# One kernel for a decaying recurrence and a gated feed-forward: its table of emission times replaced by a list scheduler, and five d_ff tiles beside the recurrence instead of four

## The chip, the cores and the metric

The kernel runs on 1 core of one Trainium2 chip. The metric is the device time of one execution in microseconds (us). Engine names in the profile: PE is TensorE's matmuls, PEld its weight loads, DVE VectorE, ACT ScalarE, POOL GpSimd, SP SyncE, which here issues the DMAs.

## The reference, cut to what matters

```python
# batch 4, 8 heads, 768 tokens, head dimension 40
for t in range(S):
    y[:, :, t] = np.einsum('bhd,bhde->bhe', rt, state)
    Sa = np.einsum('bhde,bhe->bhd', state, at)
    state = state * wt[:, :, None, :] - np.einsum('bhd,bhe->bhde', Sa, bt)
    state = state + np.einsum('bhd,bhe->bhde', vt, kt)
x = y.transpose(0, 2, 1, 3).reshape(3072, 320)
out = ((x @ w_a) * (x @ w_b)) @ w_out      # d_ff = 1536
```

The three weight matrices arrive as float64.

## The kernel before, in words

**The recurrence** ("attention") goes in 12 chunks of 64 tokens, each for 4 batches. The state passes from chunk to chunk, so the chunks' last parts come one after the other. Per chunk the stages are:

- `prep(n, b)` for each batch (L416): load the packed input `I`, two scans and `BK` on DVE, products on POOL, the transposed form `psn` and the scores `pssc` on PE, the masked scores into `TT` on DVE; behind the last batch the diagonal blocks of `TT` go out to DRAM (`nb_d`).
- `lanes(n)` (L491): the diagonal blocks of all 32 heads come back as `N`, laid over the partitions, and 31 pairs of DVE instructions (`Yt` on L504, `Y` on L507), each dependent on the one before, solve them; the result goes out through `ts_d`.
- `merge(n)` (L522): the result comes back into `TT`, and two rounds of small matmuls (`psw`, `pst`) with ACT copies give the block beside the diagonal.
- `loads(n, b)` (L556) and `main(n, b)` (L566): per batch a chain of PE products with an ACT or DVE copy behind each (`psr`, `RH`, `psu`, `UV`, `psut`, `pss`, `psg`, `G`, `psy`, `yn`, `psyt`, `xT`), with the state's update in it (`tmp` on DVE, `ST` on POOL, `psst` on PE).
- `xform(n)` (L666): the chunk's x for 256 tokens, as high and low parts (`xk`), for the feed-forward; also stored to DRAM (`xk_d`).

**The feed-forward** goes in 12 tiles of 128 of the 1536 columns (d_ff tiles). One tile for one chunk's 256 tokens is a unit, so there are 144: 16 `ab` matmuls, an ACT copy `asb`, the product `g` on DVE, its high part `gh` on ACT and low part `gl` on POOL, and later 6 `po` matmuls (`Moe.first` L312, `Moe.second` L333). The weights' float64 words are decoded to high and low parts piece by piece, six pieces to a tile (`wraw`, with DVE, ACT and POOL work; `decode` L219, `weights` L277); a last pair of DMAs (`fill_rows` L271) completes a tile's `wt`.

Four d_ff tiles (`F1 = 4`) run beside the attention, for chunks 0 to 10: 44 units. Their sums go out to DRAM (`po_d`). The other 8 tiles follow in groups of two over all chunks, for which each chunk's `xk` is loaded again (`xk2_n`, 720 KB) and its sums too (`acc`, 320 KB). The first two `xk2` and one group's weights get room on the pool of the preparation once that is done (`early` L783), the others on the pools of the attention (`late` L799), with loads spread in time (`l0`, `l1`).

**The order.** Each engine keeps the instructions in the order in which the program emits them (`InOrder`, L51), and what waits holds up what stands behind it on that engine. The order of emission comes from the table `DEF` of emission times, 16 units to a chunk: each stage of each part is put in a list of events with its time (`at` L709, `staged` L712), which is then sorted. The lanes' DVE instructions are an exception: they wait in a queue, and one is put behind each other DVE instruction (`fill_one`, L723). PSUM has four banks for the attention (`ps_at`), two for `ab` and two for `po`. In the profile almost all instructions have the line of the helper that issues them, L62.

Of the kernel before, what the change touches and what calls it, by code (L numbers as in the profile page):

```python
# [38 lines left out]
DEF = {  # L39
# [8 lines left out]
}  # L48


class InOrder:  # L51
    """An engine whose instructions keep the order in which they are given; after() comes
    behind each."""

    def __init__(self, tc, eng):
        self.tc, self.eng, self.after = tc, eng, None

    def __getattr__(self, name):
        fn = getattr(self.eng, name)

        def call(*args, **kwargs):
            r = fn(*args, **kwargs)  # L62
            self.tc.keep_in_program_order(r)
            if self.after:
                self.after()
# [16 lines left out]
    # identity for the rows of each head  # L82
# [67 lines left out]
def wkv_moe(ctx, tc, pin, rv, vn, wa, wb, wo, out):  # L150
    nc0 = tc.nc
    nc = types.SimpleNamespace(**{e: InOrder(tc, getattr(nc0, e)) for e in (
        "tensor", "vector", "scalar", "gpsimd", "sync")})
# [21 lines left out]
    # start values of the scans: 1 at the first column of each group and behind the last  # L175
# [4 lines left out]
    # strict mask s < t, on both halves of the partitions  # L180
# [7 lines left out]
    # 1 where the row belongs to head j of its group  # L188
# [11 lines left out]
    # rows of the identity: lane half p holds the rows s = 2 i + p  # L200
# [11 lines left out]
    # DRAM scratch  # L212
# [6 lines left out]
    def decode(pool, raw, rows, ncol, dst_hi, dst_lo):  # L219
        """High and low parts of float64 words, or of float32 values."""  # L220
        def t(name, dt=I32):
            return pool.tile([P, 192], dt, tag=name, name=name, bufs=2)[:rows, 0:ncol]
# [4 lines left out]
        if not WIDE:  # L227
            yield
            nc.scalar.copy(out=dst_hi, in_=shaped(raw))
            nc.vector.tensor_sub(out=dst_lo, in0=shaped(raw), in1=dst_hi.bitcast(F32))  # L230
            yield
        low, high = raw[:, :, 0], raw[:, :, 1]
        ex, mt, rs = t("w_ex"), t("w_mt"), t("w_rs")
# [6 lines left out]
        # what lies below the first 21 bits, in units of 2^-51 of the power of two  # L240
        ts(out=rs, in0=low, scalar1=1, scalar2=None, op0=ALU.logical_shift_right)
        yield
# [3 lines left out]
        stt(out=rf, in0=rs, scalar=2.0 ** -51, in1=ex.bitcast(F32), op0=ALU.mult, op1=ALU.mult)  # L246
        nc.gpsimd.tensor_sub(out=shaped(f), in0=shaped(f), in1=dst_hi.bitcast(F32))
        nc.gpsimd.tensor_add(out=dst_lo, in0=shaped(f), in1=shaped(rf))
        yield
# [3 lines left out]
    def load_piece(f, j, h):  # L253
        """Half of the columns of a d_ff tile of w_a, w_b or w_out."""
# [4 lines left out]
        if WIDE:  # L259
            raw = stage.tile([P, 192, 2], I32, tag="wraw", name="wraw", bufs=3)[:rows, 0:ncol]  # L260
            nc.sync.dma_start(out=raw.rearrange("p c x -> p (c x)"), in_=src.bitcast(I32))
        else:
            raw = stage.tile([P, 192], F32, tag="wraw", name="wraw", bufs=3)[:rows, 0:ncol]
# [3 lines left out]
    def weight_tiles(pool, i, bufs=1):  # L267
        return (pool.tile([PK, 2, 6, P], F32R, tag=f"wt{i}", name=f"wt{i}", bufs=bufs),
                pool.tile([P, 2, DM], F32R, tag=f"wo{i}", name=f"wo{i}", bufs=bufs))

    def fill_rows(wt):  # L271
        # rows of heads 6 and 7 that meet the low parts of x
# [4 lines left out]
    def weights(dest):  # L277
        """All d_ff tiles in turn, a piece per step; a step ends one piece, begins the next
        and loads the one after."""
        pieces = [(f, j, h) for f in range(NF) for j, h in PIECES]  # L280
        raw, begun = load_piece(*pieces[0]), None
        for i, (f, j, h) in enumerate(pieces):
            yield
            if begun:
                next(begun)
            following = load_piece(*pieces[i + 1]) if i + 1 < len(pieces) else None
            wt, wot = dest(f)
            if j < 2:
                v = wt[:, j, :, h * C:(h + 1) * C]
                begun = decode(stage, *raw, v[:, 0:3], v[:, 3:6])  # L290
            else:
                v = wot[:, :, h * (DM // 2):(h + 1) * (DM // 2)]
                begun = decode(stage, *raw, v[:, 0], v[:, 1])
            next(begun)
            raw = following
            if (j, h) == PIECES[-1]:
                yield
                next(begun)
                begun = None
                fill_rows(wt)  # L300
        yield
# [3 lines left out]
    class Moe:  # L305
        """Runs d_ff tiles for 256 tokens at a time; the second product of a tile comes after
# [686 lines left out]
```

## Time and profile before

| | |
|---|---|
| time, median of 3 runs | 1033.35 us (1030.91 to 1040.08) |
| span of the profiled execution, the only time its page gives | 1042.0 us |
| busy: PE, DVE, POOL, ACT | 88%, 66%, 41%, 39% |
| until chunk 3's main starts | 0 to 257.5 us |
| mains of chunks 3 to 10 | 257.5 to 668.4 us |
| main of chunk 11 | 668.4 to 725.9 us |
| seam: two more groups of instructions on PE, then PE idle from 755.0 | 725.9 to 771.2 us |
| units with nothing beside them | 771.2 to 1033.0 us |

The page cuts the span in slices; the trace can be asked for each engine's busy time in any stretch, with the clock that TensorE was granted (1.00 is full speed) and what the DMA engines moved. The stretches above were cut where the first `psr` of a chunk starts, where the last `xT` ends, and where PE stops and starts at the seam.

### The profile page before, as it was taken

How to read it: one execution, taken by the hardware profiler on the slowest of the kernel's cores; microseconds unless marked ns; L12 is line 12 of the kernel's file. 1: busy time of each engine (PE TensorE's matmuls, PEld its weight loads, DVE VectorE, ACT ScalarE, POOL GpSimd, SP SyncE). 2: the span in 40 equal slices, each digit the busy share in tenths (PEclk: the TensorE clock that was granted, in tenths of full speed). 3: DMA queues.
4: the chain of work that ended last, by engine and by line, in shares of the span. 5: the costliest groups of instructions: out<-in, count | busy, mean ns of one | idle time of the engine just before them, and what ended most of it. 6: DMA issues, size and time to landing. Idle time of an engine off the chain costs nothing.

```text
span 1042.0 us, 23609 instructions
## 1 busy us (share of the span) xinstructions
PE 915.3 (88%) x8942; PEld 832.5 (80%) x8942; DVE 692.4 (66%) x1890; ACT 411.0 (39%) x1317; POOL 426.1 (41%) x655
## 2 busy tenths in 40 slices
PE   4347798799999999999999999998939999999997
PEld 3236687688888888888888888877939999999996
DVE  7849889887869694859695937256227676757322
ACT  2122454444444444444544433345314343334221
POOL 5423647444435443434443402034215454445321
PEclk9999757889999988898989879797969999999998
DMA  3344544727364636363636242343873110110111
GB/s 72 73 103 111 119 123 106 171 58 167 99 151 113 146 100 140 82 139 115 134 104 140 84 96 85 73 133 97 202 185 88 32 43 24 39 31 25 39 57 62
DMA packets 135747, 103.29 MB, mean 99 GB/s; under 512 B 84922, under 2 KB 125690, under 8 KB 135626
## 3 DMA queue, kind: packets, MB, share of 16 engines
q1 hardware_dynamic: 135626, 101.71, 39.6%
q8 instruction: 73, 1.20, 0.5%
q14 instruction: 48, 0.39, 0.1%
HBM read 77.77 MB, written 21.94 MB: 96 GB/s over the span
## 4 chain that ended last, share of the span: by engine, by line
PE 46%; DVE 31%; DMA 9%; issue 7%; POOL 4%; ACT 2%; SPq 1%; POOLq 0%; DVEq 0%; ACTq 0%
PE ab L62 21%; PE po L62 9%; DVE Y L507 8%; DVE Yt L504 6%; PE pss L62 3%; PE psy L62 3%; DMA wraw<-in_wa_dram 2%; DVE w_ex L62 2%; DVE G L62 2%; DMA xk<-xk_d 2%; PE psr L62 2%; DVE w_rs L62 2%; DVE w_mt L62 2%; DVE TT L62 2%; SPq L62 1%
## 5 line engine op out<-in xcount | busy, mean ns | idle before, releaser
L62 PE MATMUL ab<-xk,wt 120*128 120x256 f32 x2304 | 324.2, 297 | 0.0
L62 PEld LDWEIGHTS ab<-xk,wt 120*128 120x128 f32 x2304 | 309.2, 204 | 1.2 <-DMA xk<-lo 0.3
L62 POOL TENSOR_TENSOR gl<-g,gh 128x256 fp32r<-128x256 f32 x144 | 109.6, 761 | 311.4 <-ACT gh L62 311.4
L62 DVE TENSOR_TENSOR g<-ab,asb 128x256 f32<-128x256 f32 x144 | 61.0, 424 | 158.7 <-ACT asb L62 157.0
L62 PE MATMUL po<-wo,gh 128*128 128x320 f32 x576 | 162.0, 330 | 2.8 <-ACT gh L62 2.8
L507 DVE TENSOR_TENSOR Y<-Y,Yt 128x126 f32<-128x126 f32 (+22 forms) x372 | 138.3, 372 | 8.5
L504 DVE TENSOR_TENSOR Yt<-Y,N 128x126 f32<-128x126 f32 (+22 forms) x372 | 122.7, 330 | 26.6 <-DMA N<-nb_d 19.5
L62 ACT COPY asb<-ab 128x256 f32<-128x256 f32 x144 | 53.3, 370 | 185.9 <-PE ab L62 185.9
L62 PEld LDWEIGHTS po<-wo,gh 128*128 128x128 f32 x576 | 108.6, 199 | 4.1 <-ACT gh L62 3.7
L62 ACT CAST gh<-g 128x256 fp32r<-128x256 f32 x144 | 58.5, 406 | 102.7 <-DVE g L62 98.8
L62 PE MATMUL po<-wo,gl 128*128 128x320 f32 x288 | 93.7, 325 | 2.3 <-POOL gl L62 2.3
L62 POOL TENSOR_TENSOR pe<-Pc,rp 120x192 f32<-120x192 f32 x44 | 29.4, 668 | 158.0 <-DVE rp L62 149.1
L62 PE MATMUL pssc<-Abd,BK 120*128 120x192 f32 (+1 forms) x288 | 67.5, 383 | 11.0 <-POOL Abd L62 11.0
L62 PEld LDWEIGHTS pssc<-Abd,BK 120*128 120x128 f32 x288 | 60.5, 242 | 15.4 <-POOL Abd L62 15.2
L62 DVE TENSOR_TENSOR tmp<-pss,ST 120x360 f32<-120x360 f32 x44 | 23.2, 527 | 72.3 <-PE pss L62 70.3
L62 PE MATMUL psn<-ident,BK 120*128 120x120 f32 x144 | 31.1, 336 | 38.6 <-DVE BK L62 35.2
L62 PEld LDWEIGHTS po<-wo,gl 128*128 128x128 f32 x288 | 57.7, 200 | 4.6 <-POOL gl L62 4.0
L62 PE MATMUL psy<-bkn,G 128*64 128x40 f32 x768 | 49.7, 245 | 12.2 <-DVE G L62 12.2
L62 ACT ACTIVATE w_ex<-w_ex,bias 120x192 int32<-120x192 int32 (+1 forms) x72 | 32.1, 447 | 70.8 <-DVE w_ex L62 69.7
L62 PEld LDWEIGHTS psy<-bkn,G 128*64 128x64 f32 x768 | 48.1, 161 | 14.7 <-DVE G L62 14.7
L62 POOL TENSOR_TENSOR Abd<-A,m 120x576 f32<-120x576 f32 x48 | 56.2, 1172 | 7.1 <-DVE A L62 3.2
L62 PE MATMUL psg<-rvt 120*128 120x192 f32 (+1 forms) x288 | 55.9, 334 | 0.8 <-DVE xT L62 0.8
(93 smaller groups left out, 1650.3 us busy)
## 6 DMA issues: line engine op xcount, KB each, us to landing
rvt<-in_rv_dram SPq DMA_DIRECT2D x48, 450.0 KB
I<-in_pin_dram SPq DMA_DIRECT2D x48, 361.9 KB
xk_d<-xk SPq DMA_DIRECT2D x11, 720.0 KB
xk<-xk_d SPq DMA_DIRECT2D x11, 720.0 KB
N<-nb_d SPq DMA_DIRECT2D x48, 128.0 KB
wraw<-in_wa_dram SPq DMA_DIRECT2D x24, 180.0 KB
wraw<-in_wb_dram SPq DMA_DIRECT2D x24, 180.0 KB
wraw<-in_wo_dram SPq DMA_DIRECT2D x24, 160.0 KB
```

The source lines that it names most:

```text
L62: r = fn(*args, **kwargs)
L504: lambda: nc0.vector.tensor_mul(out=Wv, in0=Y[:, 0:ni, s:s + 1].to_broadcast([P, ni, w]), in1=N[:, s:s + 1, s + 1:].to_broadcast([P, ni, w])),
L507: lambda: nc0.vector.tensor_sub(out=Y[:, 0:ni, s + 1:], in0=Y[:, 0:ni, s + 1:], in1=Wv))
```

## The change

The table, the events and the queue of lane instructions go. Every part becomes a generator that says before each step on which engine it goes on, on which tiles it waits, a claim (a time added to its readiness) and a condition (free PSUM banks, the turn among its like). The class `Order` keeps a modelled time of each engine, and a modelled time at which each tile is written, from a cost per instruction; `run` always takes the step that could start first by that model:

```diff
+    def run(self):
+        while self.parts:
+            best = None
+            for p in self.parts:
+                e, deps, claim, may = p[1]
+                if may is not None and not may():
+                    continue
+                t = max([self.now[e]] + [self.ready(x) + HOP for x in deps])
+                t += claim(t) if callable(claim) else claim
+                if best is None or t < best[0]:
+                    best = (t, p)
+            self.step(best[1])
```

This happens as the program is built. Each engine then still has one fixed order (`Issue`, in place of `InOrder`; its line is L143), and on the chip an instruction waits for its turn as before.

The parameters that move with it:

```diff
-F1 = 4         # d_ff tiles that run beside the attention
-FG = 2         # d_ff tiles of a group afterwards
+F1 = 5
+FG = 2
+NL = 10
+RAW = 3
...
+PACE = 42.0
+HOP = 0.1
+LAND = 2.1
+PER_KB = 0.0055
...
-        NL = 12
...
-            rvt_t[q] = rvt = a2.tile([PK, 21, C], F32, tag="rvt", name="rvt", bufs=3)
+        rvt_t[q] = rvt = order.tile(a2, [PK, 21, C], F32, tag="rvt", name="rvt", bufs=2)
...
-            xks[n] = xk = (mp if n == NS - 1 else a1).tile(
-                [PK, 6, B * C], F32R, tag="xk", name="xk", bufs=1)
+        xk = order.tile(mp, [PK, 6, B * C], F32R, tag="xk", name="xk", bufs=2)
```

`NL` is the number of batches that may be prepared ahead; `PACE` sets how the units of a chunk are spread over the time of one. With `F1 = 5`, 55 units run beside the attention, and the other 7 tiles follow as groups (5, 6), (7, 8), (9, 10), (11). A unit's `g`, `gh` and `gl` have three buffers each, not two, and three units may be open.

In chunk 0 the products with the state, which is zero there, are left out of `psr` and `psy`, and the zeroing of `ST`, `SD` and most of `UV` goes. The state's update is a part of its own (`self_state`), beside the rest of `main`.

The moves from the attention to the rest:

```diff
+    def early():
+        yield "sync", [], 0.1, lambda: done.prep == NS * B and done.merge == NS * B
+        pctx.close()
...
+    def late():
+        yield "sync", [], 0.0, lambda: done.y == NS * B and done.state == NS * B
+        actx.close()
+        lp[0] = lctx.enter_context(tc.tile_pool(name="xp", bufs=1, reuse_waits="tile"))
+        for n in range(NS - 1):
+            yield "sync", [], 0.0, lambda: done.moe > n
+            load_acc(n)
+            if n >= NE:
+                yield "sync", [], 0.0, None
+                load_x(lp[0], n)
...
+        for n in range(NS - 1):
+            yield from job(n, -1)
+        for n in range(NE):
+            yield from job(n, 0)
+        yield from job(NS - 1, -1)
+        for n in range(NE, NS):
+            yield from job(n, 0)
```

`job(n, -1)` are the units of chunk n with the first five tiles, `job(n, 0)` those with tiles 5 and 6.

**What the order shows, on SP, behind the attention.** The loads of the sums (`acc`, from `po_d`) and of x (`xk_n`, from `xk_d`) for the later groups, and the weight pieces (`wraw`). Before, near the end of that list:

```order
L62 DMA xk_6_9677<-xk_d_101 120x1536
L62 DMA acc_9679<-po_d_113 128x2x320
L62 DMA xk_7_9712<-xk_d_102 120x1536
L62 DMA acc_9714<-po_d_114 128x2x320
L62 DMA wraw<-in_wa_dram 120x384
L62 DMA wraw<-in_wb_dram 120x384
L62 DMA xk_8_9807<-xk_d_103 120x1536
L62 DMA acc_9814<-po_d_115 128x2x320
L62 DMA xk_9_9816<-xk_d_104 120x1536
L62 DMA acc_9818<-po_d_116 128x2x320
L62 DMA wraw<-in_wb_dram 120x384
```

Now, the end of the list:

```order
L143 DMA acc_9856<-po_d_115 128x2x320
L143 DMA xk_8_9858<-xk_d_103 120x1536
L143 DMA acc_9860<-po_d_116 128x2x320
L143 DMA xk_9_9862<-xk_d_104 120x1536
L143 DMA acc_9864<-po_d_117 128x2x320
L143 DMA xk_10_9866<-xk_d_105 120x1536
L143 DMA wraw<-in_wo_dram 128x320
L143 DMA wt_9301<-wt_9301 40x2x128 x2
L143 DMA wraw<-in_wa_dram 120x384 x2
```

`wt_9301` is tile 6, the second of the first group: its last piece and its `fill_rows` stood ahead of all these loads for the group's second tile of before (`wt_8889`), and stand behind the 11 loads of `acc` and 9 of `xk` now.

**On PE at the same place**, behind the last transposes of the attention. Before, where `wt_8887` and `wt_8889` are tiles 4 and 5 and `wo_198` tile 3 (repeated and later `po` rows are left out):

```order
L62 MATMUL psyt<-ident,yn 120x128
L62 MATMUL psyt<-ident,yn 120x64
L62 MATMUL po_0_0_9166<-wo_198,gh 128x320
L62 MATMUL po_0_0_9166<-wo_198,gl 128x320
L62 MATMUL po_0_1_9167<-wo_198,gh 128x320
L62 MATMUL po_0_1_9167<-wo_198,gl 128x320
L62 MATMUL ab_0_0_9438<-xk_0_9029,wt_8887 128x256 x16
L62 MATMUL ab_0_1_9463<-xk_0_9029,wt_8889 128x256 x16
L62 MATMUL ab_1_0_9500<-xk_1_9174,wt_8887 128x256 x16
L62 MATMUL ab_1_1_9533<-xk_1_9174,wt_8889 128x256 x16
L62 MATMUL ab_0_9574<-xk,wt_191 128x256 x16
```

Now, where `wt_9299` and `wt_9301` are tiles 5 and 6 (again without the rows that repeat):

```order
L143 MATMUL psyt<-ident,yn 120x128
L143 MATMUL psyt<-ident,yn 120x64
L143 MATMUL ab_5_9781<-xk_0_9303,wt_9299 128x256 x16
L143 MATMUL psf<-ones,tot 1x1
L143 MATMUL po_5_0_9838<-wo_9300,gh 128x320
L143 MATMUL po_5_0_9838<-wo_9300,gl 128x320
L143 MATMUL po_5_1_9839<-wo_9300,gh 128x320
L143 MATMUL po_5_1_9839<-wo_9300,gl 128x320
L143 MATMUL ab_6_9911<-xk_0_9303,wt_9301 128x256 x16
L143 MATMUL ab_5_9928<-xk_1_9305,wt_9299 128x256 x16
```

One unit stands between the attention and the first use of tile 6; the units of chunk 11 with the first tiles (`wt_191` and on) come after both chunks 0 and 1, as before.

**On PE around a merge**, in the middle of the attention; `TT_177` is the chunk that is being merged, `TT_176` the one before it. Rows between those shown are left out. Before:

```order
L62 MATMUL psw<-W,TT_177 32x32 x16
L62 MATMUL ab_2_5870<-xk,wt_195 128x256 x16
L62 MATMUL psu<-RH,TT_176 64x40 x8
L62 MATMUL psr<-ST_183,A 64x120 x2
L62 MATMUL psr<-UV_179,TT_177 64x40 x6
L62 MATMUL pst<-TT_177,W 32x32 x16
L62 MATMUL pss<-UV_182,bkn 120x120 x3
L62 MATMUL ab_3_6057<-xk,wt_197 128x256 x16
L62 MATMUL psu<-RH,TT_177 64x40 x8
```

Now:

```order
L143 MATMUL psw<-W,TT_177 32x32 x16
L143 MATMUL ab_1_6326<-xk,wt_193 128x256 x16
L143 MATMUL po_0_0_6355<-wo_192,gh 128x320
L143 MATMUL ab_2_6394<-xk,wt_195 128x256 x16
L143 MATMUL pst<-TT_177,W 32x32 x16
L143 MATMUL po_0_0_6355<-wo_194,gh 128x320
L143 MATMUL ab_3_6482<-xk,wt_197 128x256 x8
L143 MATMUL psr<-ST_183,A 64x120 x2
L143 MATMUL psr<-UV_180,TT_177 64x40 x6
L143 MATMUL psu<-RH,TT_177 64x40 x8
```

Before, the merge of a chunk stood between the last products of the chunk before it, and a unit's `ab` between stages of both. Now the main of the chunk before is over, units stand in a bunch between the rounds of the merge, and two batches of the next main go side by side behind it. Counted along PE's order, 39 units lay ahead of chunk 11's main before and 52.5 now, and 7 and 11 ahead of chunk 3's.

More of the change, by code (lines that the diff above doesn't have):

```diff
@@ L333, in second @@
-        def second(self):
-            name, gh, gl, wot, first, last, done = self.pending.popleft()
-            if first:
-                self.po = [pso.tile([P, 512], F32, tag="po", name=f"po{name}_{hf}") for hf in range(2)]
+            yield "tensor", [gl, wot], self.claim, lambda: Unit.turn[0] is self and (not self.is_first or Unit.po_free)
+            if self.is_first:
+                Unit.po_free = False
+                Unit.po = [order.tile(pso, [P, 512], F32, tag="po", name=f"po{self.name}_{hf}", bufs=2) for hf in range(2)]
@@ L888, in wkv_moe @@
-        while fill:
-            fill_one()
-        nc.vector.after = None
+        for h in ORDER:
+            if h == 6 and n:
+                r_s(2)
+            p0 = row0(h)
+            mul(ps[p0:p0 + C, h * D:(h + 1) * D], G[:, h, :], bkn[:, h, :], n == 0, n == 0 or h in (2, 5, 7))
+        done.main += 1
+        yield "scalar", [ps], 0.0, None
+        yn = order.tile(a2, [P, 2 * PK], F32, tag="yn", name="yn", bufs=2)
+        w = 2 * PK if n else 2 * PK - D
+        if n == 0:
+            nc.gpsimd.memset(yn[0:C, w:], 0.0)
@@ new lines, in xform @@
+    def xform(n):
+        yield "scalar", [], 0.0, lambda: done.y == B * (n + 1) and done.moe >= n - 1
+        x = xT_t.pop(n).rearrange("p g b t -> p g (b t)")
+        xk = order.tile(mp, [PK, 6, B * C], F32R, tag="xk", name="xk", bufs=2)
+        yield from expand(x, xk, nc.gpsimd)
+        done.x += 1
+        xks[n] = xk
+        if n < NS - 1:
+            yield "sync", [xk], 0.05, None
+            nc.sync.dma_start(out=xk_d[n], in_=xk.bitcast(F32))
+    acc = {}
+    ready_w = set()
+    ws1 = [weight_tiles(wp, i) for i in range(F1)]
@@ new lines, in wkv_moe, with all_weights, load_x @@
+    finished = set()
+    def all_weights():
+        for f in range(NF):
+            kk = (f - F1) // FG
+            if f >= F1:
+                yield "sync", [], 0.1, lambda: (
+                    len(sets) > 2 if kk == 0 else done.moe >= NS if kk < 3 else kk - 3 in finished)
+            yield from tile_weights(f, lambda: dest(f), 0.1 if f < F1 else 0.2, ())
+            ready_w.add(f)
+    def load_x(pool, n):
+        xk2[n] = order.tile(pool, [PK, 6, B * C], F32R, tag=f"xk2_{n}", name=f"xk2_{n}", bufs=1)
+        nc.sync.dma_start(out=xk2[n].bitcast(F32), in_=xk_d[n])
@@ new lines, in load_acc @@
+    def load_acc(n):
+        acc[n] = order.tile(lp[0], [P, 2, DM], F32, tag=f"acc{n}", name=f"acc{n}", bufs=1)
+        nc.sync.dma_start(out=acc[n], in_=po_d[n].rearrange("f p d -> p f d"))
+    def early():
+        yield "sync", [], 0.1, lambda: done.prep == NS * B and done.merge == NS * B
+        pctx.close()
+        ep = rctx.enter_context(tc.tile_pool(name="ep", bufs=1, side="right", reuse_waits="tile"))
+        sets.append([weight_tiles(ep, i) for i in range(FG)])
+        for n in range(NE):
+            yield "sync", [xk_d[n]], 0.1, None
+            load_x(ep, n)
@@ L892, in wkv_moe @@
+    for i in range(NU):
+        nc.gpsimd.memset(UV[i][:, H], 0.0)
+    for q in range(NS * B):
+        order.part(prep(q))
+    for n in range(NS):
+        order.part(lanes(n))
+    for q in range(NS * B):
+        order.part(loads(q))
+        order.part(main(q))
+    for n in range(NS):
+        order.part(xform(n))
+    order.part(all_weights())
+    order.part(moe())
+    order.part(early())
+    order.part(late())
+    order.part(judge())
+    order.run()
     lctx.close()
@@ L911, in all_tiles @@
             w = weight_tiles(p, "s")
[L912 removed]
             for f in range(NF):
[L914 to L917 removed]
+                for _ in tile_weights(f, lambda: w):
+                    pass
+                for _ in Unit(mp, f"s{f}", xk, w, f == 0, f == NF - 1, store).whole():
+                    pass
         token_by_token(tc, p, ps_at, pin, rv, all_tiles)
```

1013 lines of the change are left out of this document (508 added, 505 removed), and 8 rows, old and new, of the table DEF.

## The prediction

> **What bounds the kernel now.** I read the page's first part, then cut the span into stages by engine, then looked in each stage for what ends last.
>
> ```profile
> span 1042.0 us, 23609 instructions
> PE 915.3 (88%) x8942; PEld 832.5 (80%) x8942; DVE 692.4 (66%) x1890; ACT 411.0 (39%) x1317; POOL 426.1 (41%) x655
> core 0: us, PE busy (x) PEld busy (x) DVE busy (x) ACT busy (x) POOL busy (x), PEclk, DMA share, GB/s
> 0.00:257.50 257.50, 183.00 (x1675) 156.14 (x1675) 205.40 (x590) 93.32 (x316) 125.37 (x206) 0.86 0.47 110
> 257.50:668.40 410.90, 392.65 (x4535) 346.74 (x4533) 292.20 (x798) 185.12 (x635) 157.91 (x243) 0.89 0.47 113
> 668.40:725.90 57.50, 51.33 (x538) 45.06 (x537) 30.41 (x87) 26.48 (x88) 19.84 (x29) 0.86 0.42 112
> 725.90:755.00 29.10, 28.80 (x215) 28.30 (x214) 6.56 (x17) 10.25 (x27) 10.33 (x15) 0.94 0.79 187
> 755.00:771.20 16.20, 0.00 (x1) 0.03 (x2) 2.90 (x11) 1.57 (x4) 1.90 (x3) 0.65 1.00 228
> 771.20:1033.00 261.80, 257.94 (x1982) 255.26 (x1982) 153.74 (x388) 93.81 (x248) 110.06 (x159) 0.98 0.16 47
> 1033.00:1042.00 9.00, 1.56 (x7) 0.93 (x6) 1.18 (x3) 0.40 (x1) 0.73 (x1) 0.68 0.17 52
> ```
>
> Four limits, then. Until 257.5 DVE is the busiest (205.4 of 257.5). In the mains of chunks 3 to 10, 410.9 us or 51.4 a chunk, PE is busy for 392.65, but at a mean clock of 0.89: at full clock it holds 392.65 x 0.89 = 349.5 us of work. At 755.0 PE stops for 16.2 us while DMA is at 1.00. From 771.2 PE is busy all the time at 0.98.
>
> Why is the clock low in the second stage? Four neighbouring slices of 3.41 us, inside chunk 7, with the timeline's row of PE at the end of the first:
>
> ```profile
> 483.36:486.77 3.41, 2.27 (x40) 1.65 (x36) 3.29 (x6) 1.48 (x6) 1.81 (x2) 1.00 0.29 103
> 486.77:490.19 3.42, 3.42 (x28) 2.91 (x27) 3.33 (x12) 1.41 (x6) 0.69 (x2) 0.50 0.49 150
> 490.19:493.60 3.41, 3.41 (x18) 3.41 (x17) 2.49 (x5) 0.00 (x0) 3.33 (x6) 0.50 0.87 277
> 493.60:497.01 3.41, 3.41 (x27) 3.17 (x26) 2.45 (x8) 1.95 (x7) 0.77 (x2) 1.00 0.21 79
> ...
> 486.61 0.78 PE L62 MATMUL psy<-bkn,G 128*64 128x40 f32 x12 [1.14 <-DVE G L62]
> ```
>
> PE was idle for 1.14 us of the first; the next two were granted half clock although PE was full in both. So idle time of about a microsecond, here a wait for one masked product on DVE, costs some 3.4 us more behind it. That is where most of the 410.9 - 349.5 = 61.4 us goes.
>
> Beside PE runs a second chain, the lanes, on DVE:
>
> ```profile
> 257.50:668.40 410.90, 172.84 (x492) 0.89 0.47 113
> 498.41 0.19 DVE L507 TENSOR_TENSOR Y<-Y,Yt 128x16 f32<-128x16 f32 x1
> 510.96 0.19 DVE L504 TENSOR_TENSOR Yt<-Y,N 128x31 f32<-128x31 f32 x1 [1.50 <-ACT W L62]
> 549.51 0.19 DVE L507 TENSOR_TENSOR Y<-Y,Yt 128x16 f32<-128x16 f32 x1
> ```
>
> The first row is the lanes' own time on DVE, 172.84 over 8 chunks, 21.6 a chunk. The others are the end of one chunk's lanes, the next one's first instruction and its last. One chunk's lanes take 549.7 - 511.0 = 38.7, since other DVE work is put between their instructions, and the gap before them is 12.4. Together 51.1: the lanes and the chunk's period of 51.4 are one rhythm.
>
> Units by stage, from the count of `g` (a record or two missing), and the end of the chain:
>
> ```profile
> 257.50:668.40 410.90, 13.49 (x32) 13.28 (x33) 25.05 (x33) 0.89 0.47 113
> 725.90:771.20 45.30, 4.25 (x10) 4.06 (x10) 7.37 (x10) 0.84 0.86 202
> 771.20:1033.00 261.80, 37.97 (x90) 36.18 (x89) 67.42 (x89) 0.98 0.16 47
> 999.86 1.90 PE ab L62 x16
> 1027.59 1.91 PE ab L62 x16
> ```
>
> Ten units take 1027.59 - 999.86 = 27.73, so 2.77 each undisturbed; the 90 of the last stage take 261.8 / 90 = 2.91 with their small stops. PE work saved there is time saved.
>
> **The change, part by part.**
>
> *Fifth d_ff tile.* Eleven units move from the end to beside the attention. Gain at the end: counted with the seam below. Cost beside the attention: by the order, 41.5 units lie between the mains of chunks 3 and 11 where 32 lay, so 9.5 x 2.77 = 26.3 us of PE work more; 349.5 + 26.3 = 375.8 at full clock.
>
> *The mains of chunks 3 to 10.* Low end 376: PE full, never cooled. High end: the same ratio of time to work as before, 410.9 / 349.5 = 1.176, so 442. Between them stands the lanes' chain. The new order leaves one chunk's lanes nearly alone on DVE (21.6 plus about ten other instructions at 292.20 / 798 = 0.37, so 25), and puts the next one's among main and preparation, near the 38.7 of before less a little: 36. Ahead of the first kind the gap holds the round trip through DRAM, 12.4 before and about 14 now; ahead of the second it holds two batches of main and the last preparations, which I estimate at 25. That is 100 us in two chunks, 400 in eight. PE gets its units in bunches around the merge, which should leave fewer slices with a microsecond of idle time, but an `ab` of 1.90 may stand ahead of a `psr` or `psw` that is ready. I take 406, 50.8 a chunk, nearest to the period that was measured.
>
> The Trainium skill, "TensorE: Matmul & The Clock Gate", Part 1, puts the fall of the clock behind a whole idle window of about 3.4 us, and its closing table warns of gaps above about 3 us. The trace disagrees: 1.14 us of idle time in a slice was enough. By that rule the bunches would be free of any loss, and the stage would be the low end, 376.
>
> *Until chunk 3's main.* Decoding one tile more costs DVE 32.00 / 4 = 8 us here, by this row, and POOL and ACT work too:
>
> ```profile
> 0.00:257.50 257.50, 32.00 (x96) 0.86 0.47 110
> ```
>
> Four units more go to PE, 11 us, into 74 us of idle time. Against that, chunk 0's zeroing and state products go. If DVE's work is on the path, 257.5 + 8 = 266; if the list scheduler packs DVE better (52 us are idle now), 250. Ordering by readiness should recover part: 260.
>
> *Main of chunk 11.* 2.5 units fewer, 7 us: high end 50.5. At full clock 51.33 x 0.86 - 7 = 37. No lanes run beside it any more, but no units fill its waits: 44.
>
> *The seam.* This speaks against the change. Before, PE had 29.1 us of units behind the attention (10 by the count above) and then stood for 16.2. The chain there:
>
> ```profile
> 735.10 18.86 DMA xk<-xk_d
> 754.02 16.25 DMA wraw<-in_wa_dram
> 770.29 0.26 DVE w_ex L62
> DMA packets 3205, 8.10 MB, mean 225 GB/s; under 512 B 252, under 2 KB 2332, under 8 KB 3203
> q1 hardware_dynamic: 3203, 8.08, 99.5%
> xk<-xk_d SPq DMA_DIRECT2D x11, 720.0 KB
> acc<-po_d SPq DMA_DIRECT2D x11, 320.0 KB
> ```
>
> From 735 to 771 the one queue moved 8.10 MB at 225 GB/s, and a weight piece issued at 754.0 landed at 770.3 behind loads of x. In the new order all 11 `acc` and 9 `xk` loads go out in one pile as the attention ends: 11 x 320 + 9 x 720 = 10000 KB, 10.24 MB, so 45.5 us at 225 GB/s. Behind the pile on SP stand tile 6's last piece and the DMAs that complete `wt_9301`. PE has one unit with tile 5 (2.8 us) and then needs `wt_9301`; everything else, chunk 11's units too, is queued behind that on PE. PE restarts 45.5 + 1.5 = 47 us after the attention; the 1.5 is an estimate for the last decode and the small DMAs, where the steps from 770.29 to PE's start at 771.20 took 0.9. At the 277 GB/s of the fastest slice quoted it would be 38.5, at the 187 of the row from 725.9, 56. The old seam took 45.3 for 10 units; the new one takes 47 for one. So the nine units that it does not do, about 26 us, are what it costs, and this eats most of the fifth tile's 11 units.
>
> *The rest.* 55 units beside the attention and one in the seam leave 88 x 2.91 = 256. Small costs: two `rvt` buffers in place of three and ten prepared batches in place of twelve can make loads late, inside the 376 to 442 above; the second `xk` buffer and third `g` only loosen. The tail stays 9.0.
>
> *Sum on the profiled span:* 260 + 406 + 44 + 47 + 256 + 9 = 1022, against 1042.0. That execution lies 1042.0 - 1033.35 = 8.65 above the median of its three runs (1030.91 to 1040.08), so I expect a median of 1013.
>
> **The rivals.**
>
> 1. *PE bound.* The bunches keep the clock up and PE is the limit in the mains: 376 to 385 in place of 406, and 37 in the last main. For it: DVE has 410.9 - 292.2 = 119 us idle in that stage. Against it: the lanes' chain, 100 in two chunks. Time: 1013 - 25 - 5 = 983.
> 2. *The fixed order meets the lanes.* The model's times are not the chip's. With `psr` and `psw` queued behind bunches of units and the units behind a `psw` that waits for late lanes, PE idles over a microsecond several times a chunk and each time runs at half clock after it. At the ratio of before the mains take 442 and the last 50.5: 1013 + 36 + 6.5 = 1055. For it: every wait of PE in the old order was already filled by a unit placed there, and the loss was still 15%. Against it: two batches of main now go side by side. It turns the change into a loss from 1033.35 on, that is from 20 us more in the mains, a period of 53.3.
> 3. *The pile does not hold PE*, because its first loads go out well before the attention ends or tile 6's DMAs pass it: the seam costs the 16.2 of before plus one unit, 19 in place of 47: 1013 - 28 = 985. For it: the last chunk makes no state, so part of the attention's room is free before its end. Against it: the order on SP, and that the room is the attention's own.
>
> The page "DMA: Bandwidth & Descriptors" of the Trainium skill, "Queues, rings and completion order", says that each ring of a queue takes its descriptors in order but that completion is not in order; by the first half tile 6's piece waits for the pile, by the second the last rows may pass it a little. The 16.25 us of the weight piece above agrees with the first.
>
> **How the numbers follow.** Forecast (within 20 us of 1013) 0.45; rival 1 0.17; rival 2 0.20; rival 3 0.08; no net change, with several of these cancelling, 0.10. About 1%, 1023.0 to 1043.7, is what a measurement of this kernel can tell from no change. Two thirds of the forecast's share (0.30), rivals 1 and 3 (0.25) lie below: 0.55. Between lie 0.12 of the forecast, a quarter of rival 2 (0.05) and most of the rest (0.08): 0.25. Above lies 0.20. The range leaves a tenth on each side: 972, near rival 1 with part of rival 3, to 1050, inside rival 2. The forecast's own range is 995 to 1032.
>
> **What would show it.** Right: no unit of tile 6 in the seam until about 47 us after the last `xT`, PE idle for some 40 of it with DMA near 1.00; the first `psr` of chunks 3 to 11 about 50.8 apart on average, alternately shorter and longer; a clock above 0.89 there; 88 units in the last stage at 2.9. Wrong: a seam under 25 us, a period under 48.5 or over 53.3, a first stage outside 250 to 266, or PE idle in the last stage because `acc` or `xk` come late.

## The result: slower by 6%

The changed kernel takes 1094.3 us in the median (1087.19 to 1097.9, 4 runs), the kernel before 1032.1 beside it: 1.060 times as long, 95% interval 1.052 to 1.068. The forecast was 1013 with a range from 972 to 1050. Below, times are medians of all runs, ratios to the kernel before leave slow runs out, and the profiled executions of four experiments (decode spread, chunk 0 first, preparations later, and the kernel before with `l1` at 4.0) lie 5 to 20 us above their medians, so their stretches are upper values.

The page of the changed kernel, its first lines and the slices of PE and its clock:

```profile
span 1095.5 us, 23444 instructions
PE 902.9 (82%) x8894; PEld 820.6 (75%) x8894; DVE 683.8 (62%) x1878; ACT 411.4 (38%) x1317; POOL 417.8 (38%) x659
...
PE   3328788588989989999979989998705999999997
...
PEclk8655756769897989789978989898956999999998
```

PE does no more than before (902.9 against 915.3) in a span that is 53.5 us longer. Cut at the same places (the first `psr` of chunk 3 and of chunk 11, the last `xT`, PE's stop and start):

```profile
core 0: us, PE busy (x) PEld busy (x) DVE busy (x) ACT busy (x) POOL busy (x), PEclk, DMA share, GB/s
0.00:292.70 292.70, 195.25 (x1832) 171.49 (x1832) 226.95 (x639) 108.12 (x360) 134.26 (x235) 0.70 0.45 106
292.70:746.70 454.00, 419.43 (x4763) 368.31 (x4762) 288.83 (x790) 190.50 (x646) 161.98 (x246) 0.90 0.46 104
746.70:784.60 37.90, 34.16 (x352) 29.67 (x351) 21.11 (x64) 18.59 (x64) 11.87 (x19) 0.86 0.48 119
...
788.50:833.30 44.80, 1.99 (x11) 1.70 (x10) 3.31 (x10) 1.11 (x3) 3.36 (x6) 0.51 0.99 213
833.30:1086.50 253.20, 248.45 (x1924) 246.76 (x1924) 138.81 (x367) 90.06 (x240) 102.64 (x149) 0.99 0.12 36
```

| stretch | before | forecast | after |
|---|---|---|---|
| until chunk 3's main | 257.5 | 260 | 292.7 |
| mains of chunks 3 to 10 | 410.9 | 406 | 454.0 |
| main of chunk 11 | 57.5 | 44 | 37.9 |
| from there to the end | 316.1 | 312 | 310.9 |

The end came as forecast, the seam with it. PE's wait there, and the chain through it:

```profile
PE ab L143 <- DMA wt<-wt: 43.5, 1, 43.5
```

```profile
786.91 18.21 DMA acc<-po_d
805.12 0.02 issue
805.14 14.96 DMA acc<-po_d
820.10 0.02 issue
820.12 13.88 DMA wt<-wt
834.00 0.04 issue
834.04 6.13 PE ab L143 x27
```

PE waits 43.5 us for the DMAs that complete tile 6, behind the pile. By these cuts the losses lie ahead of it: 35.2 us until chunk 3's main and 43.1 us in the mains, with 19.6 us won back in the main of chunk 11.

The cuts, at the first `psr` of a chunk, do not compare like with like, though. Here are the last `xT` (the end of the main) of chunk 2 and of chunk 10, before and now:

```profile
275.74 0.35 DVE L62 TENSOR_TENSOR xT<-psyt,pe 120x192 f32<-120x192 f32 x1
...
686.18 0.36 DVE L62 TENSOR_TENSOR xT<-psyt,pe 120x192 f32<-120x192 f32 x1 [4.76 <-PE psyt L62]
```

```profile
267.77 0.35 DVE L143 TENSOR_TENSOR xT<-psyt,pe 120x192 f32<-120x192 f32 x1
...
729.86 0.36 DVE L143 TENSOR_TENSOR xT<-psyt,pe 120x192 f32<-120x192 f32 x1 [2.55 <-PE psyt L143]
```

Before, two mains overlap: chunk 2 ends (276.1) 18.6 us behind the first `psr` of chunk 3. Now it ends (268.1) 24.6 us ahead of it. Counted by chunks that are done, the changed kernel is 8.0 us ahead after chunk 2, then takes 462.1 us for chunks 3 to 10 where 410.4 passed (51.7 more), and 14.9 us more for chunk 11. So nothing is lost up to the end of chunk 2; what is lost is the overlap of one main with the next, and time in every chunk behind it.

**Where the mains lose it.** DVE's rows of the timeline with the lanes of two chunks, first and last instruction of each:

```profile
402.91 0.19 DVE L143 TENSOR_TENSOR Yt<-Y,N 128x31 f32<-128x31 f32 x1 [1.35 <-DMA N<-nb_d]
...
425.20 0.19 DVE L143 TENSOR_TENSOR Y<-Y,Yt 128x16 f32<-128x16 f32 x1
...
475.16 0.18 DVE L143 TENSOR_TENSOR Yt<-Y,N 128x31 f32<-128x31 f32 x1
...
509.80 0.18 DVE L143 TENSOR_TENSOR Y<-Y,Yt 128x16 f32<-128x16 f32 x1
```

Lanes of 22.5 us and of 34.8, near the 25 and 36 forecast; but the gap between them is 49.8, where 25 was estimated. And PE's rows at the merge of the chunk whose lanes ended at 425.20:

```profile
457.82 0.81 PE L143 MATMUL psw<-W,TT 32*32 32x32 f32 x32
...
461.76 1.27 PE L143 MATMUL psw<-W,TT 32*32 32x32 f32 x32
...
468.17 0.67 PE L143 MATMUL psr<-ST,A 120*64 120x120 f32 x4
468.76 0.87 PE L143 MATMUL psr<-UV,TT 64*64 64x40 f32 x12
```

Its first `psw` runs 32 us after its lanes. So it is in chunks 4, 6 and 8 (30 to 32 us); in the kernel before it came 7 to 14 us after them in every chunk. What can stand there is seen around chunk 3's merge, just ahead of this stretch:

```profile
273.02 1.43 DVE L143 STREAM_TRANSPOSE W<-TT 32x640 f32<-32x640 f32 x2 [2.46 <-DMA TT<-ts_d]
```

```profile
269.61 2.15 PE L143 MATMUL ab<-xk,wt 120*128 120x256 f32 x16
274.97 3.78 PE L143 MATMUL ab<-xk,wt 120*128 120x256 f32 x16 [3.21 <-DVE g L143]
...
283.38 0.81 PE L143 MATMUL psw<-W,TT 32*32 32x32 f32 x32
284.12 2.18 PE L143 MATMUL ab<-xk,wt 120*128 120x256 f32 x16
```

`psw`'s operand `W` was there at 274.5. PE, in its fixed order, first does an `ab` that waits 3.21 us for a `g`, itself behind that `W` on DVE, and takes 3.78 us where others take 2.2; then come the bunch's `po`, and it reaches `psw` at 283.4.

### The profile page after: what moved, and what is told of

It reads as the page before. It is cut to its first block, busy times and chain, and to the rows that moved or that the text cites. A ratio compares the mean times of both kernels' runs of the same rounds, so it can differ in the third digit from the quotient of the medians.

```text
span 1095.5 us, 23444 instructions
## 1 busy us (share of the span) xinstructions
PE 902.9 (82%) x8894; PEld 820.6 (75%) x8894; DVE 683.8 (62%) x1878; ACT 411.4 (38%) x1317; POOL 417.8 (38%) x659
## 5 line engine op out<-in xcount | busy, mean ns | idle before, releaser
L143 PE MATMUL ab<-xk,wt 120*128 120x256 f32 x2304 | 326.5, 296 | 47.2 <-DMA wt<-wt 43.5
L143 PEld LDWEIGHTS ab<-xk,wt 120*128 120x128 f32 x2304 | 306.9, 202 | 50.0 <-DMA wt<-wt 43.8
L143 POOL TENSOR_TENSOR gl<-g,gh 128x256 fp32r<-128x256 f32 x144 | 108.9, 758 | 284.7 <-ACT gh L143 284.4
L143 PE MATMUL po<-wo,gh 128*128 128x320 f32 x576 | 160.9, 326 | 8.3 <-ACT gh L143 6.6
L143 DVE TENSOR_TENSOR g<-ab,asb 128x256 f32<-128x256 f32 x144 | 60.4, 420 | 157.0 <-ACT asb L143 156.6
L143 DVE TENSOR_TENSOR Y<-Y,Yt 128x126 f32<-128x126 f32 (+22 forms) x372 | 126.3, 340 | 11.4
L143 DVE TENSOR_TENSOR Yt<-Y,N 128x126 f32<-128x126 f32 (+22 forms) x372 | 112.0, 301 | 25.5 <-DMA N<-nb_d 14.4
L143 PE MATMUL pssc<-Abd,BK 120*128 120x192 f32 (+1 forms) x288 | 70.9, 399 | 60.2 <-POOL Abd L143 39.9
L143 PEld LDWEIGHTS po<-wo,gh 128*128 128x128 f32 x576 | 106.1, 194 | 12.7 <-ACT gh L143 9.4
L143 ACT COPY asb<-ab 128x256 f32<-128x256 f32 x144 | 53.7, 373 | 156.3 <-PE ab L143 155.8
L143 PEld LDWEIGHTS pssc<-Abd,BK 120*128 120x128 f32 x288 | 63.0, 250 | 64.7 <-POOL Abd L143 64.1
L143 PE MATMUL po<-wo,gl 128*128 128x320 f32 x288 | 94.6, 329 | 12.6 <-POOL gl L143 12.2
L143 ACT CAST gh<-g 128x256 fp32r<-128x256 f32 x144 | 58.5, 407 | 86.6 <-DVE g L143 84.5
L143 POOL TENSOR_TENSOR ST<-tmp,pcm 120x360 f32<-120x360 f32 x40 | 32.9, 822 | 102.1 <-DVE tmp L143 100.2
L143 PEld LDWEIGHTS po<-wo,gl 128*128 128x128 f32 x288 | 56.2, 195 | 20.0 <-POOL gl L143 19.7
L143 ACT ACTIVATE w_ex<-w_ex,bias 120x192 int32<-120x192 int32 (+1 forms) x72 | 32.3, 449 | 96.5 <-DVE w_ex L143 95.5
L143 PE MATMUL psr<-UV,TT 64*64 64x40 f32 x768 | 55.3, 254 | 13.7 <-DMA UV<-in_vn_dram 13.6
L143 DVE TENSOR_SCALAR w_ex<-wraw 120x192 int32<-120x192 int32 (+1 forms) x72 | 32.4, 450 | 53.5 <-DMA wraw<-in_wo_dram 41.9
L143 PEld LDWEIGHTS psr<-UV,TT 64*64 64x64 f32 x768 | 43.5, 159 | 28.0 <-DMA UV<-in_vn_dram 15.2
L143 POOL TENSOR_TENSOR Abd<-A,m 120x576 f32<-120x576 f32 x48 | 57.9, 1206 | 10.3 <-DVE A L143 6.9
L143 POOL TENSOR_TENSOR w_mt<-w_mt,wt 120x192 f32<-120x192 f32 x48 | 29.7, 618 | 80.6 <-ACT wt L143 40.7
L143 POOL TENSOR_TENSOR pe<-Pc,rp 120x192 f32<-120x192 f32 x44 | 24.4, 555 | 89.8 <-DVE rp L143 83.1
```

## The experiments

For the mains, four readings stood against each other: the fifth tile's work, units counted overdue too early (`PACE`), the rank of the merge, and ten prepared batches in place of twelve (`NL`).

**Four tiles** (`F1 = 5` to `4`).

> The changed kernel with four d_ff tiles beside the attention, not five; the list scheduler and all else stay. Measured so far: the mains of chunks 3 to 10 take 454.0 us in the changed kernel and 410.9 before, the stretch ahead of them 292.7 and 257.5. Theory LOAD (the fifth tile's PE and DVE work is what lengthens both): mains fall to 411 to 425, the first stretch to about 270, total about 1045 to 1060. Theory ORDER (the order of merge, units and main costs the time whatever the load): mains stay at 440 or more and the first stretch above 280; the 11 units that come back to the end cost 30 there, so the total is 1090 to 1120.

1129.5 us, 1.095 of before (1.084 to 1.106): slower still. ORDER by the stretches, and 9 above its range in total. The mains take 469.3 with less work in them; the first stretch 288.6.

**Tile 6 ahead of the pile.**

```diff
+        ... done.state == NS * B and F1 + 1 in ready_w
```

> The changed kernel; only the pile of acc and x loads behind the attention now waits until tile 6's weights have been issued. Theory SEAM (the 44.8 us in which PE waits is tile 6's last piece behind the pile): the wait falls to under 15 us and the total by 25 to 35, to about 1060 to 1070. Rival (bandwidth: 10.24 MB have to come in any case): PE stops a little later for chunk 2's x or sums, and the total falls by less than 10.

1075.3 us, 1.043 (1.034 to 1.052): 19 lower, between the two. PE's wait for tile 6's DMAs fell to 3.8, but another of 18.7 came behind it (see the paced loads).

**PACE 70.**

> The changed kernel with PACE 70 in place of 42, so that a chunk's units are counted overdue later and seldom go ahead of a merge or main that is ready. Theory PACE (overdue units ahead of a ready psw are what lengthens the period of 56.8): period 50 to 53, total 1050 to 1070. Rival LOOP (merge stands behind the whole of the main before, so period is main plus merge, units or not): period 55 to 58, total within 10 of 1094.

1091.5 us, 1.061 (1.052 to 1.070). LOOP: the mean period went from 56.8 to 55.1 only, and the first stretch grew to 302.1. The mains lost 13.2 of their 43.1 us, with two units fewer in them, so PACE is at most a part of the cause.

**Four tiles and NL 12.**

> As the run with four d_ff tiles, and NL back from 10 to 12 prepared batches. Theory BUFFERS (ten prepared batches hold up the second preparation of each pair of chunks, so that periods alternate near 53 and 63): the alternation goes, the mains are 25 us or more below the run with four tiles and NL 10. Rival: the alternation comes from somewhere else and the two runs agree within 10.

1115.2 us, 1.084 (1.074 to 1.093). The mains fall from 469.3 to 439.4: BUFFERS, as far as it goes. With ten prepared batches, end of one chunk's lanes and start of the next one's:

```profile
254.70 0.19 DVE L143 TENSOR_TENSOR Y<-Y,Yt 128x16 f32<-128x16 f32 x1
...
298.30 0.19 DVE L143 TENSOR_TENSOR Yt<-Y,N 128x31 f32<-128x31 f32 x1 [4.81 <-DMA N<-nb_d]
```

With twelve:

```profile
257.29 0.19 DVE L143 TENSOR_TENSOR Y<-Y,Yt 128x16 f32<-128x16 f32 x1
...
274.95 0.19 DVE L143 TENSOR_TENSOR Yt<-Y,N 128x31 f32<-128x31 f32 x1 [0.89 <-DMA N<-nb_d]
...
312.64 0.19 DVE L143 TENSOR_TENSOR Y<-Y,Yt 128x16 f32<-128x16 f32 x1
```

The gap of 43.4 is 17.5: with ten, the last preparations of a chunk wait, by the condition in `prep`, for the second batch's main two chunks back. Of the later gaps six are 12 to 20, but one of 45.8 is left. And that next chunk's `psw` still comes at 342.67, 30 us after its lanes.

**Merge first** (and the sums' reload waits for its store, as this order needs it).

```diff
-            yield "tensor", [W], urgent, lambda: done.at > 1
+            yield "tensor", [W], -0.05, lambda: done.at > 1
```

> As the run with four tiles and NL 12 (1115 us, mains of chunks 3 to 10 in 439.4), and the merge's matmuls and copies now go ahead of mains and units whenever they are ready (claim -0.05 in place of 0.05); also the sums' reload waits for its store, which the new order needs. Theory PRIORITY (psw stands 17 to 30 us behind the end of the lanes because mains and overdue units are emitted first): psw comes 8 to 12 us behind the lanes' end, mains of chunks 3 to 10 fall to 370 to 405, total 1060 to 1085. Rival LATENCY (two batches of main side by side take 40 us a chunk and PE idles in them at half clock, wherever the merge stands): mains fall by less than 10 and the clock stays at or below 0.85.

1084.5 us, 1.055 (1.044 to 1.065), 31 below the run without it. PRIORITY, at the upper end of its numbers: `psw` of the same chunk comes 12.6 after its lanes, no gap between lanes in this stretch is over 24, and the mains take 405.7, as long as in the kernel before (410.9, and 404.4 with its loads paced, below), at a clock of 0.91:

```profile
326.53 0.81 PE L143 MATMUL psw<-W,TT 32*32 32x32 f32 x32
```

```profile
294.50:700.20 405.70, 382.16 (x4484) 334.03 (x4483) 283.22 (x758) 182.23 (x626) 151.82 (x237) 0.91 0.50 115
```

**Merge first with five tiles and NL 10.**

> The changed kernel (five tiles, NL 10) with the merge ahead of mains and units, as before tried with four tiles and NL 12, where it took 33 us off the mains; the sums' reload waits for its store. Theory PRIORITY ALONE: mains of chunks 3 to 10 fall from 454.0 to 415 to 430, total 1060 to 1070. Rival BOTH NEEDED (with ten prepared batches every second chunk's lanes start late and that chunk waits for them whatever the merge's rank): the long periods near 63 stay, mains fall by less than 15, total above 1080.

1128.4 us, 1.093 (1.089 to 1.097). BOTH NEEDED, and worse than that: 34 above the changed kernel. The mains grew from 454.0 to 483.4, at a clock of 0.84 in place of 0.90; why they grew is not shown. The gap ahead of every second chunk's lanes stays, 44.5 here:

```profile
430.50 0.19 DVE L143 TENSOR_TENSOR Y<-Y,Yt 128x16 f32<-128x16 f32 x1
...
475.21 0.18 DVE L143 TENSOR_TENSOR Yt<-Y,N 128x31 f32<-128x31 f32 x1
```

```profile
291.20:774.60 483.40, 450.06 (x4771) 394.91 (x4769) 294.48 (x800) 190.74 (x652) 162.38 (x247) 0.84 0.43 99
```

**The scheduler's PE costs times 1.2.**

> The changed kernel; the scheduler's costs of all PE instructions are multiplied by 1.2, so that its modelled PE is about as slow as the chip's at a mean clock of 0.85; also the sums' reload waits for its store. Theory MODEL (the fixed order is wrong because it was made for a PE at full clock): mains of chunks 3 to 10 at 435 or less in place of 454, first stretch below 285, total 15 or more lower. Rival: the order's faults come from its rules (claims, ten prepared batches), and mains and total stay within 10.

1156.4 us, 1.125 (1.112 to 1.137). MODEL falls: the mains grew to 498.6. A PE cost nearer the chip's mean did not give a better order.

For the seam:

**All of this together, and the pile behind tile 5.**

> As the run with four tiles, NL 12 and the merge first, and the pile of loads waits until tile 5's weights, the second of the first group, have been issued; the sums' reload needs no condition of its own here. If the seam's cost is independent of the mains, it is 15 to 25 below that run. Rival: with the mains shorter or longer the pile meets other loads, and the difference is below 8.

1079.1 us, 1.048 (1.039 to 1.057): only 5 lower, the rival. PE's longest wait behind the attention:

```profile
PE ab L143 <- DVE g L143: 25.2, 2, 24.7
```

The chain shows why: the pile now delays the next group's first weight piece, and on DVE the decode that waits for it stands ahead of a unit's `g`.

```profile
785.09 17.44 DMA wraw<-in_wa_dram
802.52 0.02 issue
802.55 0.27 DVE w_ex L143
```

**Paced loads.**

```diff
+            yield "sync", [], 0.0, lambda: done.moe > n and Unit.stored > n and n <= done.g0 + 3
```

> As the run with four tiles, NL 12, merge first and tile 5 ahead of the pile (1079 us, in which PE still stood 24.7 us behind a g that stands behind a decode that waits for a raw weight behind the pile). Now the loads for chunk n go out only once the units of chunk n - 3 have begun. Theory QUEUE (weight pieces wait behind the pile in the one queue): no wait of PE over 8 us behind the attention, total 1055 to 1065. Rival BANDWIDTH: x and sums come late instead, and the total is within 8 of 1079.

1055.1 us, 1.021 (1.018 to 1.024), 24 lower. QUEUE. No wait of PE behind the attention is over 1.0; in the 50 us behind it PE is busy for 46.7:

```profile
748.30:798.30 50.00, 46.69 (x346) 44.85 (x346) 26.78 (x73) 19.20 (x52) 21.72 (x32) 0.98 0.92 219
```

**Five tiles with all of it** (room for `NL = 12` from one `xk` buffer).

> Five tiles with all that was mended: NL 12 (room for it from one xk buffer in place of two), merge first, tile 6 ahead of the pile, paced loads. Against the same with four tiles: theory LOAD: the fifth tile's 9.5 units cost 26 us in the mains and give back 29 to 32 at the end, total within 8. Rival: with one xk buffer and more DVE work the mains lose 40 or more and the total is 10 to 40 higher.

1106.8 us, 1.073 (1.066 to 1.079), 52 above four tiles. The rival, and more than it said: the mains take 477.9 against 408.6, and 454.0 in the changed kernel. `psw` now comes 8 to 15 us behind the lanes in every chunk, but two gaps between lanes, of 48.9 and 46.8, are left. How much of it is the fifth tile and how much the single `xk` buffer was not separated.

For the first stretch:

**Decode later** (tile 0's from chunk 0's lanes on).

> The changed kernel; decoding of the first weight tile begins only when chunk 0's lanes are done. Theory DECODE (the decode ahead of chunk 0's lanes is what costs the first stretch): chunk 0's main starts at 72 to 77 in place of 86.5, chunk 3's at 280 or earlier in place of 292.7, total 10 to 20 lower. Rival (DVE has to do it anyway, and it stretches the lanes of chunks 1 and 2 instead): chunk 3's main at 288 or later, total within 8.

1115.1 us, 1.083 (1.073 to 1.093). The rival, and 21 worse: chunk 0's main starts at 81.3, chunk 3's at 315.1.

**Decode spread**, tile f from modelled time 40 + 40 f.

> As the run with paced loads, and the decode of the first four weight tiles is spread: tile f gives way to the lanes until modelled time 40 + 40 f, then goes ahead. Theory LANES (decode put between the dependent lane instructions stretches the lanes of chunks 1 and 2 to 59 and 63 us, 35 and 52 before, and that is what makes the first stretch 298 and not 257.5): the lanes of chunks 1 and 2 last 30 to 50, chunk 3's main starts at 265 to 285, total 15 to 30 lower than with paced loads alone. Rival LOAD: DVE's work is the same and the first stretch stays above 290.

1058.7 us, 1.016 (1.010 to 1.022), where the paced loads alone gave 1.021. The lanes of chunks 1 and 2 last 33.1 and 53.4 us, yet chunk 3's main starts at 289.5. LANES falls as it was put.

**Chunk 0 first**, **no decode**, **preparations later** and **chunk 0 first with the decode spread**:

> As the run with paced loads (1055 us, chunk 0's main at 93.9, chunk 3's at 290.9); preparations from the ninth batch on and all decoding now wait until chunk 0's merge is in the order. Theory AHEAD (DVE does 72 us of work before chunk 0's main where 50 were done before, four preparations and a weight tile too many, and that delay is never made up): chunk 0's main starts at 70 to 76 and chunk 3's 12 to 20 earlier than 290.9. Rival CONSERVED (the work has to be done before chunk 3's main in any case): chunk 0's main is as early, but chunk 3's stays within 8 of 290.9.

> As the run with paced loads, with work left out: the first four weight tiles are neither loaded nor decoded, and the units beside the attention multiply with one tile of zeros; all else runs as before. Theory DVE (decode between the lanes' instructions sets the first stretch): chunk 3's main starts at 215 to 250 in place of 290.9. Rival HALF CLOCK (PE's chain of main and merge, at a clock of 0.7, sets it): 270 or later.

> As the run with paced loads; only the preparations from the ninth batch on wait for chunk 0's merge, the decode does not. Theory AHEAD: chunk 0's main at 78 to 84, chunk 3's 5 to 12 earlier than 290.9. Rival CONSERVED: chunk 3's main within 5 of 290.9.

> As the run that puts chunk 0 first, with the decode spread: tile f gives way to the lanes until modelled time 75 + 35 f. If both are needed (chunk 0 early and lanes free of decode), chunk 3's main starts at 265 to 280 and the total is 1030 to 1045. Rival CONSERVED: 285 or later.

1085.1, 1027.5, 1061.3 and 1080.9 us (1.049, 1.039 to 1.059; 0.992, 0.984 to 1.000; 1.025, 1.015 to 1.035; 1.046, 1.037 to 1.054). With chunk 0 first its main starts at 69.9, with the preparations later at 78.5; chunk 3's still at 294.4 and 295.1: CONSERVED, AHEAD falls; nor is either ratio below the 1.021 of the paced loads. Without the decode chunk 3's main starts at 240.0. DVE is busy for 159.25 us in that stretch, against 219.61 in the run with paced loads:

```profile
0.00:240.00 240.00, 174.75 (x1723) 153.64 (x1723) 159.25 (x443) 81.46 (x296) 89.40 (x163) 0.69 0.44 100
```

```profile
0.00:290.90 290.90, 182.63 (x1794) 160.85 (x1794) 219.61 (x619) 99.15 (x335) 124.26 (x217) 0.69 0.42 99
```

60.4 us less on DVE brought 50.9. But the run also leaves out the weights' loads and their work on ACT and POOL (POOL's row falls from 124.26 to 89.40), so it shows the decode as a whole, and not DVE's share of it. And the mains of chunks 3 to 10 grew from 408.6 to 435.7, so half of the gain was given back. With chunk 0 first and the decode spread, chunk 3's main came at 265.9, as early as this scheduler got with all its work, but the mains took 455.0, with a gap of 70.6 between two chunks' lanes. What causes that gap is not shown.

**The kernel before, its loads paced**: one number of its table, `l1` from 2.78 to 4.0 and 5.0.

> The kernel before with one number of its table changed: the loads of x and sums behind the attention are spread, 4.0 units of emission time from chunk to chunk in place of 2.78. Theory QUEUE: PE's wait of 16.2 us behind the attention falls to under 8, the time falls by 8 to 14 us. Rival BANDWIDTH: x comes late for the units instead, and the time stays within 4.

> As the run before it with 5.0 units, close to the 5.08 at which two units of a chunk are emitted, so a load stands just ahead of the unit that needs it. Theory QUEUE: the wait of 16.2 goes, but each chunk's units may wait some us for its x (720 KB at 225 GB/s is 3.3 us): the time falls by 4 to 14. Rival BANDWIDTH: no gain or a loss.

1022.7 and 1021.1 us, 0.993 (0.989 to 0.997) and 0.993 (0.990 to 0.997): the only versions with all their work that are faster than both kernels, by under 1%. QUEUE by the wait: PE's 16.3 us are 4.5 with 4.0 and 3.8 with 5.0. By the time 5.0 is inside its range and 4.0 falls short of the 8 to 14. Behind the attention 303.1 us pass with 5.0 where 316.1 did:

```profile
PE psf L62 <- DVE tot L62: 3.8, 1, 3.8
```

```profile
717.00:1020.10 303.10, 287.66 (x2203) 283.66 (x2201) 164.31 (x417) 106.02 (x280) 123.15 (x178) 0.98 0.28 72
```

The gain on the median, 6 to 7, is half of that; where the other half goes is open.

This number moves nothing ahead of the seam, and the stretches there are 255.5, 404.4 and 57.1 with 5.0, where the kernel before had 257.5, 410.9 and 57.5: differences of some 6 us in the mains are not a finding.

## Why the prediction was wrong, point by point

**The work was right, what is lost beside it was not.** PE's busy time by its clock, and the rest of the stretch, for the mains of chunks 3 to 10:

| kernel | length | busy x clock | the rest |
|---|---|---|---|
| before | 410.9 | 349.5 | 61.4 |
| changed | 454.0 | 419.43 x 0.90 = 377.5 | 76.5 |
| four tiles | 469.3 | 409.88 x 0.84 = 344.3 | 125.0 |
| four tiles, NL 12 | 439.4 | 403.96 x 0.85 = 343.4 | 96.0 |
| the same, merge first | 405.7 | 382.16 x 0.91 = 347.8 | 57.9 |
| five tiles, NL 10, merge first | 483.4 | 450.06 x 0.84 = 378.0 | 105.4 |

375.8 was forecast for the changed kernel's work and 377.5 measured. The forecast of 406 left 30 us for the rest, and it is 76.5.

**The step that failed in the mains** is the lanes' chain, "That is 100 us in two chunks". Three of its four terms held: lanes of 22.7 and 35.4 us on average, where 25 and 36 were taken, and gaps of 12.7 to 18.3, where 14 was. The gap of 25 ahead of every second chunk's lanes was an estimate with no row behind it; it is 40.5, 49.8 and 44.0 (chunks 5, 7 and 9). With four tiles its cause is shown: `NL = 12` takes the mains from 469.3 to 439.4. The prediction had put ten prepared batches among the "small costs". A second step is missing, the merge: the prediction allowed for one `ab` of 1.90 ahead of a ready `psw`, while in chunks 4, 6 and 8 `psw` stood 30 to 32 us behind the lanes. With four tiles and `NL = 12`, merge first takes the mains from 439.4 to 405.7.

For the changed kernel itself, with five tiles, these two causes are argued and not shown. Merge first alone made its mains longer (483.4), and both mends together, with a single `xk` buffer, left them at 477.9 with two long gaps. `NL = 12` alone was not run with five tiles.

**Rival 2** was what happened in the mains, at 454 in place of 442: PE waits behind a fixed order and runs at half clock after it. Its break-even, a period of 53.3, is passed with 56.8. It had 0.20. It did not foresee the first stretch, and its 1055 is 39 short. (Rival 1's sum takes 5 us off for the last main, where its own 37 in place of 44 gives 7.)

**The first stretch**, 260 forecast, 292.7 measured. "Ordering by readiness should recover part" is the step that failed. The 35.2 us over the kernel before are three pieces: chunk 3's lanes end at 262.7 and not 243.6 (19.1), its `psw` comes 20.7 and not 9.2 us behind them (11.5), and 9.3 and not 4.7 us pass from there to the `psr` (4.6). The forecast also took this cut for a measure of progress, which it is not: chunk 2 was done 8.0 us earlier than before. One term was mis-sized: the row of `wraw` counts four of the six DVE instructions of a piece. The other two (`w_mt<-w_ex,w_mt` and `w_rs<-w_rs,w_ex`) have 19.8 us beside its 32.0, so a tile's decode is 51.8 / 4 = 13 us on DVE and not 8. But the fifth tile is only 4.1 of the 35.2 (292.7 against 288.6). DVE does 66.2 us of work before chunk 0's main where it did 49.8, and that main starts at 86.5 and not 71.4; moving work behind it did not bring chunk 3's forward. Which rules of the order would have to change is left open; the old table does the same decode of four tiles in 257.5.

**The seam** held: 47 forecast from the last `xT` to PE's start, 48.7 measured, and the rule of order in the queue with it. Its cost, 26, was about right: in the kernel with four tiles, 5.4 and 24.0 came back with tile 5 ahead of the pile and the loads paced.

**Main of chunk 11**: 37.9, near the low end of 37 and not the 44 taken, but by luck. That low end meant 37 us of work at full clock; PE does 34.16 x 0.86 = 29.4 there, since chunk 10's main no longer reaches into this stretch.

## What to carry to other kernels

A list scheduler's fixed order is only as good as its rules: here, as the runs with four tiles show, the merge, the head of the next chunk's chain, had a weaker rank than mains and overdue units, and too few prepared buffers made every second chunk late. Cut two kernels at finished work before you say where one loses: the first instruction of a stage is no such mark when one kernel overlaps its stages and the other does not. Price a change of order by the chain that carries state, with a row for every gap in it, and count what PE loses to idle time and half clock, not only its work. Bulk loads that are not needed yet should be paced to their use: in one queue they hold up the small transfer that is needed next, and an in-order engine hands that wait on.

## What the runs showed of the hardware that was not expected

The granted clock reads 1.00 at the start of the kernel before, where PE in fact ran at half clock. Six `pssc` matmuls there, and the same six later in a slice at 1.00:

```profile
0.00:71.40 71.40, 27.48 (x206) 22.90 (x206) 49.80 (x132) 14.69 (x50) 28.86 (x59) 1.00 0.33 69
```

```profile
9.03 2.07 PE L62 MATMUL pssc<-Abd,BK 120*128 120x192 f32 x6 [1.15 <-POOL Abd L62]
...
494.65 1.04 PE L62 MATMUL pssc<-Abd,BK 120*128 120x192 f32 x6
```

2.07 against 1.04: the column is to be trusted only where durations agree. So the first stretch's mean clocks, 0.86 before and 0.70 after, are not to be compared.

What the forecast read from one place about idle time holds through the mains of chunks 3 to 10 of the kernel before. In slices of 3.41 us, the clock fell from 1.00 to 0.50 behind 15 of them; in 14 of these 15 PE was idle for 0.57 to 1.89 us, and behind no slice with more than 0.76 us of idle time did the clock stay at 1.00.
